# A delta-rule kernel with a GELU network behind it: the first group's 32x32 inverses by halves, and two chunks' K work moved

## The chip, the cores and the metric

The kernel runs on one core of a Trainium2 chip. The time is device time of one execution, in microseconds (us). The engines are PE (TensorE, matrix products), DVE (VectorE), ACT (ScalarE), POOL (GpSimd) and SP (SyncE, which issues most of the transfers).

## The reference

Four batches of eight heads run the delta rule over 768 steps with vectors of 48, and the result, with the heads side by side, goes through two matrix products with an exact GELU between them.

```python
# q, k, v: (4, 8, 768, 48), beta: (4, 8, 768)
k_n = k / (np.linalg.norm(k, axis=-1, keepdims=True) + 1e-06)
for t in range(S):
    y[:, :, t] = einsum('bhd,bhde->bhe', q[:, :, t], state)
    v_old = einsum('bhde,bhd->bhe', state, k_n[:, :, t])
    state = state + beta_t * einsum('bhd,bhe->bhde', k_n[:, :, t], v[:, :, t] - v_old)
x = y.transpose(0, 2, 1, 3).reshape(3072, 384)
h = x @ w_in                     # 384 -> 2048
g = 0.5 * h * (1 + erf(h / sqrt(2)))
out = g @ w_out                  # 2048 -> 384
```

The weights arrive as 64-bit floats (two 32-bit words each) and are turned into 32-bit floats on the core.

## The kernel before

**Chunks.** The 768 steps are cut into 12 chunks of 64. In a chunk the recurrence is a triangular system per head: the Gram products of the keys, scaled, make a strictly lower triangular 64x64 matrix; its inverse (`Zf`) applied to the values (`W`) gives `U` (`solve`), from which follow the output (`use`, `read`) and the next state (`update`, `next_state`). A chunk has two tiles ("units", one per pair of batches), a group two chunks, so 32 inverses of 64x64 per half of the partitions. Chunk 0 has no state before it, so its `W` needs no product with the state (`against_state` is one multiply on POOL there).

**The inverse.** The diagonal 32x32 blocks of a group are laid side by side by a transpose on DVE (`flip`, line 482), scaled (line 487), and inverted in place by elimination: for j = 1 to 30 a product of a column with a row (line 494) and an add (line 496), each instruction waiting for the one before. Then two 32x32 inverses become a 64x64 one (`join`, lines 531 to 556): level 0 multiplies the block below the diagonal (`Gs`, here G) by one inverse, level 1 by the other. `XM` holds the inverse turned one way, `Zf` the other; `back` (lines 502 to 509) turns them on DVE.

**The network.** Chunk c's rows, turned (`turn`), go through `fc1` (16 tiles f of the first layer, psH) and `fc2` (psO), the latter adding over f. In chunk 0 the first layer runs while the pieces of w_in are decoded: `begin`, `exponents`, `mantissas` and `signed` work on DVE and ACT, one piece per two tiles f, eight for w_in, then eight for w_out; pieces 0 to 2 have one DVE instruction more (line 260) than 3 to 7. The psH tiles share two PSUM buffers, each freed by a GELU on ACT.

**The order.** Up to `by_hand.close()` (line 1138) the program order is written out by hand for all engines: the chunk 0 and 1 products, the elimination of the first group (`rows`, line 1099), the join and chunk 0's recurrence. While DVE eliminates, PE does the query products of chunks 0 and 1 and, from line 1089 on, the K transposes, Grams and Q transposes of chunks 2 and 3. After it a list of steps with due times (`plan`, in chunk numbers: 1.25 is a quarter into chunk 0's network) sets DVE's order; a scheduler orders PE and ACT from what each instruction waits for. There `join` of chunk 1 stands at 1.085 and 1.16, chunk 1's recurrence at 1.31 to 1.58 (`state_at(1, ...)`), the loads of chunk 3 at 0.98. SP issues transfers in order, and each waits for its buffer.

Of the kernel before, what the change touches and what calls it, by code (L numbers as in the profile page):

```python
# [19 lines left out]
def kernel(  # L20
# [179 lines left out]
    slots = [su.tile([128, 2 * WG], U32, tag=f"w_raw{i}", name="w_raw", bufs=1) for i in range(3)]  # L200
# [329 lines left out]

    def join(g, ts, level, copy=nc.scalar.copy):
# [149 lines left out]
    def solve(us, copies=(nc.scalar.copy, nc.scalar.copy)):  # L681
        psU = dn("psU")
        for u in us:
            zf = Zf[(u.c // 2) % 2]
# [368 lines left out]
    for n in range(2):  # L1053
        fetch(n)
    load_k(2, "Kp")
    new_group(0)
# [3 lines left out]
    for u in first:  # L1060
        squares(u, n0[:, u.t], nc.gpsimd if u.t == 1 else nc.vector)
        transposed(u, (0,))
        if u.t in (1, 2):
            diagonals(first[u.t - 2 + 1])
    diagonals(first[2])
    signs(0, 2)
    diagonals(first[3])
    root(n0)
    scales_, flip_, *rows, back0, back1, back2, clear_ = [s_[1:] for s_ in eliminate_steps(0)]
    factors(gms[0], beta_m[:, 0:2].rearrange("q c a h -> q (c a) h"), n0)  # L1070
    scales_[0]()
    flip_[0]()
# [4 lines left out]
    for u in first:  # L1077
        transposed(u, (1,))
        queries([u])
    for a in range(NA):  # L1080
        fetch_in(tiles[2, a].Qp[:, :, 0:D], q, tiles[2, a])
    for a in range(NA):
        fetch_in(Qp[2 + a][:, :, 0:D], k, tiles[3, a])
    for n in range(2, NS):
        fetch(n)
    for n in range(n_in, n_in + len(slots)):
        fetch(n)
    load_v(1)
    third = [tiles[2, a] for a in range(NA)]
    for u in third:  # L1090
        transposed(u, (0,))
    grams(third)
    for u in third:
        transposed(u, (1,))
    fourth = [tiles[3, a] for a in range(NA)]
    for u in fourth:
        transposed(u, (0,))
    grams(fourth)
    for fn, *args in rows:
        fn(*args)  # L1100
    nc.vector.scalar_tensor_tensor(ng, gms[0][:, 0:NA], -1.0, ns[0], ALU.mult, ALU.mult)
    back0[0](*back0[1:])
    against_state(first[:NA])
    for u in first:
        masked(u)
    back1[0](*back1[1:])
    for a in range(NA):
        join(0, (a,), 0)
    back2[0](*back2[1:])
    for a in range(NA):  # L1110
        join(0, (a,), 1)
    clear_[0](*clear_[1:])
# [5 lines left out]
    begin(1)  # L1118
    mantissas(1)
    solve(first[:NA])  # L1120
    exponents(1)
    signed(0)
    use(first[:NA])
    for u in first[:NA]:
        read(u)
# [170 lines left out]
```

## Time and profile before

| | |
|---|---|
| median of 3 runs | 646.93 us (646.61 to 647.02) |
| the profiled execution | 647.82 us, its span 645.8 us |
| PE busy in the span | 621.7 us (96%) |
| DVE busy | 499.2 us (77%) |
| ACT busy | 260.3 us (40%) |
| POOL busy | 63.4 us (10%) |
| chunk 0's first layer (psH) starts | 57.64 us |
| second layer (psO) starts | 90.40 us |

Lines of a timeline give start and length in us, the engine, the source line, the operation, what is written from what, the form, and in brackets how long the engine had been idle before and what released it. A group's line gives count, total time, the mean of one in ns and the idle time before. A chain's line gives start, length, engine, what, and the line. Records of PE count the passes of 32-bit products, so one 32-bit matmul makes two records and one transpose makes one.

### The profile page before, as it was taken

To read this page: it belongs to the slowest core of one execution; us is meant where nothing else is said; L and a number is where in the kernel's file an instruction comes from. 1 tells how busy PE (TensorE), PEld (TensorE's weight loads), DVE (VectorE), ACT (ScalarE), POOL (GpSimd) and SP (SyncE) were. 2 spreads that over 40 slices of the span, in tenths; PEclk is the share of its full clock that TensorE was granted. 3 is DMA by queue.
4 is the path that set the end of the run, shared out by engine and by line. 5 is a ranking of instruction groups with operands and counts; after the bars stand their busy time and mean duration, and the time that the engine had idled before them with its cause. 6 is when DMAs were issued, how large, how long until landed. Compare 5 with 4: busy or idle time off the path is not lost.

```text
span 645.8 us, 22160 instructions
## 1 busy us (share of the span) xinstructions
PE 621.7 (96%) x9702; PEld 574.4 (89%) x9702; DVE 499.2 (77%) x1023; ACT 260.3 (40%) x586; POOL 63.4 (10%) x58
## 2 busy tenths in 40 slices
PE   6769999999999999999999999999999999999997
PEld 5657776776699999999999999999999999999997
DVE  6999889989799997999677999677999565354342
ACT  3366777625352157132156132166132253132230
POOL 4041004100311004001004001003001000000000
PEclk9976999999899999999999999999999999999999
DMA  9795654303433235321425312412211300100101
GB/s 129 178 272 170 127 159 138 50 1 69 63 59 46 53 44 88 54 30 31 70 34 84 60 25 36 71 18 38 51 25 34 67 5 3 25 2 2 26 3 24
DMA packets 158433, 39.79 MB, mean 62 GB/s; under 512 B 150016, under 2 KB 153216, under 8 KB 158336
## 3 DMA queue, kind: packets, MB, share of 16 engines
q1 hardware_dynamic: 155344, 36.94, 29.5%
q10 hardware_dynamic: 2992, 1.43, 1.1%
q8 instruction: 76, 1.25, 0.8%
q14 instruction: 21, 0.17, 0.1%
HBM read 33.62 MB, written 4.72 MB: 59 GB/s over the span
## 4 chain that ended last, share of the span: by engine, by line
PE 86%; DVE 8%; ACT 2%; issue 2%; DMA 1%; ACTq 0%; SPq 0%; DVEq 0%
PE psX L834 12%; PE psY L889 11%; PE psX L889 8%; PE psY L834 7%; PE psO L804 7%; PE psH L786 6%; PE psV L889 5%; PE psZ L889 5%; PE psZ L834 4%; PE psV L834 4%; PE psK L660 3%; PE psG L414 3%; PE psJ L586 2%; DVE tmp L494 2%; DVE Nu L496 2%; PE psU L690 2%
## 5 line engine op out<-in xcount | busy, mean ns | idle before, releaser
L494 DVE TENSOR_TENSOR tmp<-Nu 128x30 f32<-128x30 f32 (+9 forms) x180 | 62.0, 345 | 4.7
L496 DVE TENSOR_TENSOR Nu<-Nu,tmp 128x30 f32<-128x30 f32 (+9 forms) x180 | 60.3, 335 | 6.2
L889 PE MATMUL psX<-xT,w_in_sb 128*128 128x128 f32 x480 | 64.6, 277 | 0.5 <-DVE p L986 0.4
L889 PEld LDWEIGHTS psX<-xT,w_in_sb 128*128 128x128 f32 x480 | 58.8, 192 | 1.9 <-issue 0.7
L877 ACT COPY xT<-psX 128x768 f32<-128x768 f32 x9 | 7.2, 799 | 124.3 <-PE psX L763 124.3
L834 PE MATMUL psX<-w_out_sb,G 128*128 128x192 f32 x320 | 55.3, 326 | 0.0
L351 POOL TENSOR_TENSOR n<-n,half 128x16 f32<-128x16 f32 x10 | 29.9, 2986 | 258.8 <-DVE n L349 205.4
L834 PEld LDWEIGHTS psX<-w_out_sb,G 128*128 128x128 f32 x320 | 52.1, 190 | 0.0
L804 PE MATMUL psO<-w_out_sb,G 128*128 128x384 f32 x128 | 46.4, 508 | 0.0
L786 PE MATMUL psH<-xT,w_in_sb 128*128 128x256 f32 x192 | 44.6, 386 | 1.9 <-ACT G L877 1.8
L786 PEld LDWEIGHTS psH<-xT,w_in_sb 128*128 128x128 f32 x192 | 36.1, 192 | 8.7 <-ACT G L877 2.9
L889 PE MATMUL psY<-xT,w_in_sb 128*128 128x128 f32 x320 | 42.3, 275 | 0.0
L877 ACT COPY pu<-psZ 128x512 f32<-128x512 f32 x40 | 23.5, 587 | 39.2 <-PE psZ L889 39.2
L889 PEld LDWEIGHTS psY<-xT,w_in_sb 128*128 128x128 f32 x320 | 38.9, 192 | 0.0
L804 PEld LDWEIGHTS psO<-w_out_sb,G 128*128 128x128 f32 x128 | 24.1, 196 | 14.9 <-issue 1.7
L877 ACT ACTIVATE G<-G 128x512 f32<-128x512 f32 x40 | 25.2, 630 | 18.6 <-DVE G L920 17.8
L376 POOL TENSOR_TENSOR V<-V,n 128x384 f32<-128x384 f32 x18 | 16.0, 898 | 133.5 <-DMA V<-in_v_dram 131.9
L834 PE MATMUL psY<-T,G 128*128 128x192 f32 x160 | 28.6, 332 | 0.0
L834 PE MATMUL psZ<-T,pu 128*128 128x192 f32 x160 | 28.6, 332 | 0.0
L912 DVE TENSOR_TENSOR psY<-psY,pu 128x512 f32<-128x512 f32 x20 | 14.0, 698 | 18.0 <-PE psY L889 18.0
L834 PE MATMUL psV<-w_out_sb,G 128*128 128x192 f32 x160 | 27.7, 326 | 0.0
L834 PE MATMUL psX<-T,G 128*128 128x192 f32 x160 | 27.6, 326 | 0.0
(178 smaller groups left out, 1347.3 us busy)
## 6 DMA issues: line engine op xcount, KB each, us to landing
Kp<-in_k_dram SPq DMA_DIRECT2D x76, 96.0 KB, 3.3
w_out_sb<-in_moe_w_in_dram SPq DMA_DIRECT2D x24, 256.0 KB, 4.5
w_raw<-in_moe_w_out_dram SPq DMA_DIRECT2D x16, 384.0 KB, 4.4
V<-in_v_dram SPq DMA_DIRECT2D x48, 96.0 KB, 3.1
out_dram<-o_sb SPq DMA_DIRECT2D x36, 96.0 KB, 2.2
Qp<-in_q_dram SPq DMA_DIRECT2D x64, 32.0 KB, 2.1
Qp<-in_q_dram SPq DMA_DIRECT2D x16, 96.0 KB, 3.9
Qp<-in_k_dram SPq DMA_DIRECT2D x32, 32.0 KB, 2.3
```

Source lines behind the costliest of these rows:

```text
L351: nc.gpsimd.tensor_tensor(flat, flat, half, op=ALU.pow)
L376: engine.tensor_tensor(u.V, u.V, ns[u.c][:, u.a].unsqueeze(2).to_broadcast([128, H, D]), op=ALU.mult)
L414: nc.tensor.matmul(psG[HALF[p], r, i * NP + j, :], lhsT=u.Kt[rows, p, j, :], rhs=(u.Qt if x else u.Kt)[rows, p, j, :], start=True, stop=True)
L494: nc.vector.tensor_tensor(tmp, nu[:, j + 1:, j:j + 1].to_broadcast([128, n, j]), nu[:, j:j + 1, 0:j].to_broadcast([128, n, j]), op=ALU.mult)
L496: nc.vector.tensor_tensor(nu[:, j + 1:, 0:j], nu[:, j + 1:, 0:j], tmp, op=ALU.add)
L660: nc.tensor.matmul(u.psK[to, x, r, j, :], lhsT=(u.Qt if x else u.Kt)[rows, p, j, :], rhs=St[rows, u.a, p ^ r, j, :], start=True, stop=True)
L786: nc.tensor.matmul(psH, lhsT=w_in_sb[:, f // 2, m, f % 2 * 128:(f % 2 + 1) * 128], rhs=xTs[c][:, m, :], start=(m == 0), stop=(m == NM - 1))
L804: nc.tensor.matmul(u.psO, lhsT=G[:, u.a, f, :], rhs=w_out_sb[:, f, :], start=(f == 0), stop=(f == NF - 1))
L834: nc.tensor.matmul(ps_, lhsT=lhs[:, f, :], rhs=rhs[:, f, :], start=first and f == 0, stop=f == FH - 1, skip_group_check=not first)
L877: tc.keep_in_program_order(fn(*args, **kw))
L889: nc.tensor.matmul(ps_[:, i], lhsT=lhs[:, f // 2, f % 2 * 128:(f % 2 + 1) * 128], rhs=rhs, start=first and i == 0, stop=True, skip_group_c ...
L912: nc.vector.tensor_tensor(L1["Y1"], L1["Y1"], L1["pu"][:, 0], op=ALU.add)
```

## The change

The first group alone gets a new inverse. Its 32x32 blocks are cut into 16x16 squares. A tile `N0`, zeroed at the start, holds both squares of a block, and `eliminate_first` runs j = 1 to 14 on the two at once (two free dimensions more in the access pattern). The block between the two squares is then joined by PE: `below` (one 32x16 product per block), `below_out` (a multiply into `M`, whose other half is zero), `corner` (two kinds of products, psB and psC), `corner_out` and `corner_turned` (adds on DVE into `XM` and `Zf`, two copies on ACT). `corner_turned` also fills the left half of `Zf`, which was a transpose (`back`, x = 2). After that `join` runs as before.

Around it the hand-written order changes. The clears of `Zf` go from POOL to ACT, early. Only the first group's chunk 0 is joined at once; chunk 1's `below` is put behind chunk 0's solve, its corner and its join into the plan (1.005 to 1.16). `solve` of chunk 0 gets a PSUM tile for each unit, and unit 1's copies of U and x go to DVE. Unit 1's state update moves behind the turns. Pieces 1 and 2 of w_in are decoded after the recurrence, piece 1 no longer before it. The K transposes, Grams and Q transposes of chunks 2 and 3, and the query product and mask of chunk 1's second unit, move out of the hole under the elimination into chunk 0's first layer (1.1 to 1.27). On SP all four first pieces of w_in and the values of chunk 1 are fetched before chunk 2's keys; w_out's three first raw pieces share their third buffer with `N0` and wait for it; the loads of chunk 3 go from 0.98 to 1.3.

```diff
-    for n in range(2):
+    for n in range(NS):
         fetch(n)
+    load_v(1)
     load_k(2, "Kp")
+    prepare_first()
...
+        if u.t == 0:
+            clear_first(0, 0)
+            clear_first(0, 1)
+        elif u.t == 2:
+            clear_first(1, 0)
...
-    scales_[0]()
-    flip_[0]()
+    scales_first()
+    flip_first()
...
-    for u in first:
-        transposed(u, (1,))
-        queries([u])
+    transposed(first[0], (1,))
+    transposed(first[1], (1,))
+    queries(first[0:1])
+    transposed(first[2], (1,))
+    queries(first[1:2])
     for a in range(NA):
         fetch_in(tiles[2, a].Qp[:, :, 0:D], q, tiles[2, a])
+    for j in range(1, HS - 1):
+        eliminate_first(j)
+    back_first(0)
+    below(0)
+    back_first(1)
+    slots += [su.tile([128, 2 * WG], U32, tag=f"w_raw{i}", name="w_raw", bufs=1) for i in range(3)]
+    for n in range(n_in, n_in + len(slots)):
+        fetch(n)
+    for u in first[:NA]:
+        masked(u)
+    below_out(0)
+    nc.vector.scalar_tensor_tensor(ng, gms[0][:, 0:NA], -1.0, ns[0], ALU.mult, ALU.mult)
+    against_state(first[:NA])
+    queries(first[2:3])
+    masked(first[2])
+    corner(0)
+    corner_out(0)
+    corner_turned(0)
+    for a in range(NA):
+        join(0, (a,), 0)
+    for a in range(NA):
+        join(0, (a,), 1)
+    transposed(first[3], (1,))
     for a in range(NA):
         fetch_in(Qp[2 + a][:, :, 0:D], k, tiles[3, a])
...
-    third = [tiles[2, a] for a in range(NA)]
-    for u in third:
-        transposed(u, (0,))
-    grams(third)
-    for u in third:
-        transposed(u, (1,))
-    fourth = [tiles[3, a] for a in range(NA)]
-    for u in fourth:
-        transposed(u, (0,))
-    grams(fourth)
-    for fn, *args in rows:
-        fn(*args)
...
-    solve(first[:NA])
-    exponents(1)
+    solve(first[:NA], (nc.scalar.copy, nc.vector.tensor_copy), True)
+    below(1)
     signed(0)
     use(first[:NA])
-    for u in first[:NA]:
-        read(u)
-    signed(1)
+    update(first[0])
+    below_out(1)
+    read(first[0])
+    read(first[1], nc.vector.tensor_copy)
     for u in first[:NA]:
         turn(u)
-    for u in first[:NA]:
-        update(u)
+    update(first[1])
+    begin(1)
     begin(2)
+    exponents(1)
     exponents(2)
+    mantissas(1)
+    signed(1)
     mantissas(2)
     signed(2)
     begin(3)
...
-    plan += [at(0.98, 0.985, [(1.0, load, 3)]),
+    plan += [at(1.3, 1.305, [(1.0, load, 3)]),
+             at(1.005, 1.006, [(1.0, corner, 1)]),
+             at(1.05, 1.051, [(1.0, corner_out, 1), (1.0, corner_turned, 1)]),
+             at(1.1, 1.101, [(1.0, queries, first[3:4]), (1.0, masked, first[3])]),
+             at(1.12, 1.17, gram_steps(2)), at(1.18, 1.23, gram_steps(3)),
+             at(1.25, 1.27, [(1.0, transposed, u, (1,)) for u in third]),
              [(t, (join, 0, range(NA, 2 * NA), level)) for level, t in enumerate((1.085, 1.16))],
```

The new steps that it calls:

```python
def eliminate_first(j):
    nu = squares_of(first_["nu"])            # both 16-squares: 128 x 2 x 16 x 16
    n = HS - 1 - j                           # HS = 16
    ...
    nc.vector.tensor_tensor(tmp, nu[:, :, j + 1:, j:j + 1].to_broadcast([128, 2, n, j]),
                            nu[:, :, j:j + 1, 0:j].to_broadcast([128, 2, n, j]), op=ALU.mult)
    nc.vector.tensor_tensor(nu[:, :, j + 1:, 0:j], nu[:, :, j + 1:, 0:j], tmp, op=ALU.add)

def below(c):                                # FOUR: the four quarters of the partitions
    ps_ = first_["psA", c] = ps.tile([128, NA * H, HS], F32, tag="mlp", name="psA")
    for i, u in enumerate(range(units_of(c).start, units_of(c).stop)):
        for rows in FOUR:
            nc.tensor.matmul(ps_[rows, i, :], lhsT=Ds[0][rows, u, :], rhs=XMs[0][rows, u, 0:HS],
                             start=True, stop=True)

def corner(c):
    ...
    for i, u in enumerate(range(units_of(c).start, units_of(c).stop)):
        for rows in FOUR[::2]:
            nc.tensor.matmul(psB[rows, i, :], lhsT=zf[rows, u, HB:C], rhs=m[rows, u, 0:HS],
                             start=True, stop=True)
    for i, u in enumerate(range(units_of(c).start, units_of(c).stop)):
        for rows in FOUR:
            nc.tensor.matmul(psC[rows, i, :], lhsT=m[rows, u, :], rhs=zf[rows, u, HB + HS:C],
                             start=True, stop=True)

def corner_out(c):
    us, xm, zf = units_of(c), XMs[0], Zf[0]
    for rows in FOUR[::2]:
        nc.vector.tensor_tensor(xm[rows, us, 0:HS], xm[rows, us, 0:HS],
                                first_["psB", c][rows], op=ALU.add)
```

## The prediction

> **What bounds the kernel now.** I read the slices of the span first, then the chain in order of time, then the timelines of PE, DVE and ACT around it, then the groups by form for the price of one instruction. Slices (16.1 us each):
>
> ```profile
> PE   6769999999999999999999999999999999999997
> ...
> DVE  6999889989799997999677999677999565354342
> ...
> PEclk9976999999899999999999999999999999999999
> ```
>
> PE is full from the fourth slice to the end. So the kernel is its opening, about 58 us in which PE is not full, plus a long stretch of PE work. A change of the opening is worth what it moves the start of that stretch, less the PE work it adds. The chain in order of time tells what the opening waits for:
>
> ```profile
> 14.11 1.98 DVE Nu L482
> ...
> 17.44 0.22 DVE tmp L494
> ...
> 39.19 0.19 DVE Nu L496
> ...
> 39.49 2.12 DVE XM L505
> ...
> 47.98 2.07 PE psU L690 x61
> ...
> 57.71 4.46 PE psH L786 x18
> ```
>
> The elimination (lines 494 and 496, 60 instructions end to end) holds 17.44 to 39.38; from its end to the first solve (psU) it is 8.6 us, and 9.7 more to the first layer (psH). PE's timeline gives the marks and the clock:
>
> ```profile
> 31.36 1.97 PE L393 MATMUL psT<-ident,Kp 128*128 128x128 f32 x8
> ...
> 34.91 1.09 PE L393 MATMUL psT<-ident,Qp 128*128 128x128 f32 x8
> 38.08 1.97 PE L393 MATMUL psT<-ident,Qp 128*128 128x128 f32 x8 [2.07 <-ACT Qt L394]
> ...
> 44.45 1.96 PE L541 MATMUL psJ<-Zf,XM 32*32 32x32 f32 x64 [0.81 <-DVE XM L552]
> 47.98 2.03 PE L690 MATMUL psU<-W,Zf 64*64 64x48 f32 x64 [1.57 <-issue]
> ...
> 66.02 1.20 PE L541 MATMUL psJ<-Zf,XM 32*32 32x32 f32 x64
> ...
> 82.04 1.15 PE L690 MATMUL psU<-W,Zf 64*64 64x48 f32 x64
> ...
> 86.89 1.56 PE L786 MATMUL psH<-xT,w_in_sb 128*128 128x256 f32 x6 [0.92 <-ACT G L877]
> ...
> 90.40 1.56 PE L804 MATMUL psO<-w_out_sb,G 128*128 128x384 f32 x4
> ...
> 174.37 0.60 PE L393 MATMUL psT<-ident,Qp 128*128 128x128 f32 x4
> ...
> 176.56 1.16 PE L414 MATMUL psG<-Kt 48*64 48x64 f32 x64
> ```
>
> Eight transposes take 1.97 us at 31.36 and at 38.08, 1.09 at 34.91; so the granted 1.00 shown for the first slices is not to be believed, and the opening runs mostly at half clock. The joins and the solve show the same factor (psJ 1.96 against 1.20, psU 2.03 against 1.15). From 90.40, where the second layer begins, PE never stops until 160, in both orders of instructions. I forecast where that mark goes; what follows it is the same work in almost the same order, and shifts with it.
>
> **1. The elimination.** The 30 steps go; 14 steps on two 16-squares at once come, j = 1 to 14 with 28, 52, 72, 88, 100, 108, 112 elements and back.
>
> ```profile
> L487 DVE TENSOR_TENSOR Nu<-Nu,XM 128x1024 f32<-128x1024 f32 x1 | 1.2, 1224 | 0.1
> ...
> L494 DVE TENSOR_TENSOR tmp<-Nu 128x108 f32<-128x108 f32 x2 | 0.5, 271 | 0.1
> ...
> L494 DVE TENSOR_TENSOR tmp<-Nu 128x30 f32<-128x30 f32 x2 | 0.4, 198 | 0.1
> ```
>
> With 0.03 to 0.04 us between instructions, a pair of 30 elements takes 0.49 us, one of 108 takes 0.61; the seven sizes give 3.9, twice that 7.8, against 21.9. The scaling is two products of 256 (0.45 each, between the 0.41 of 240 elements and a quarter of 1.22) for 1.24. It starts at 14.11 as now, since that waits for ACT's diag copy at 14.08; so it ends at 24.9 instead of 39.4. Three memsets and a reduction (about 1.7 us by the 0.70 of 768 elements) fit DVE's 1.96 us wait for Kp. The four clears of Zf (0.63 each on ACT, for three of 0.69 on POOL and one on ACT) fall into ACT's waits of 1.27, 0.67 and 1.03 us between 6 and 13.7: nothing, unless a K copy is late.
>
> **2. The joins.** XM's transpose (2.13) ends at 27.1. Then new: 64 products 32x16 (128 records), a multiply (0.45), 32 and 64 products (192 records), two adds (0.44) and one (0.45), two ACT copies (0.62). A record's price is not in the trace: psD, four tiles at once, 13 ns; psJ, two tiles, 18 at full and 33 at half clock. I take 13 for the four-tile products and 16 for the others: 1.7 and 2.6 us; ends 1.7 to 4.2 and 2.5 to 6.3. So psA is done at 28.9, M at 29.6, the corner at 32.5, then both old join levels with their four multiplies (0.44) and four copies (0.37): first solve at 36.2 at full clock, 38.0 at half, against 47.98. One transpose of 1.93 is gone. POOL's scaling of the mask is half of its 1.91 and is done before the flip. POOL's masks of chunk 0 now stand ahead of W, from 26 to 28.5, and W waits for ng at 29.7: hidden.
>
> **3. To the first layer.** Chunk 0's U and x copies go half to DVE, one update moves behind the turn; but psA of chunk 1 (1.7) and its corner (2.5) come in on PE, and on DVE 0.95 + 0.95 of copies and a multiply. psH starts at 45.3 (full) to 50 (half) against 57.64.
>
> **4. The new gate.** PE does four tiles of the layer (1.40 each, by 2.79 us for 12 records) and then waits in order for chunk 1's join, which needs chunk 1's corner added on DVE. DVE must first decode pieces 1, 2 and 3: from the x copy at 41.6 on 0.95 + 1.46 + 1.85 + 1.46 + 1.85 + 0.47, the state 0.95, then 1.46 + 0.5 + 0.92, and the adds 0.9: 54.4 at full clock. At half clock the x copy is at 44.7 and the exponents of piece 1 cost 0.8: 58.2. Behind that wait stand queries, transposes, Grams and eleven more tiles' worth of layer; the layer tile f3 waits too, as its PSUM waits for a Gelu that ACT has behind the exponents of piece 3 (at 52). So the 12 us won at psH mostly run into this gate.
>
> **5. The moved K and Gram.** Four K transposes, two Grams, two Q transposes and a query product leave the hole under the elimination for a full PE. By the rows at 174.37 (0.55 from start to start) and 176.56 (1.1): 2.2 + 2.2 + 1.1 + 0.55 = 6.0 us. From the gate to the second layer PE has 12 tiles x 1.40 + joins 2.26 + 6.0 + psK 2.0 + psU 1.1 + psY 1.9 = 30.1 us. ACT gets their copies too: 4 + 2 + 4 + 1 at 0.59, 4 at 0.62, and two turned: 10.2 us on top of 23.5 busy in the 32.8 us from 57.6 to 90.4. Setting the two orders side by side, PE waits three or four times for a copy or a Gelu, 2.9 us in all (2.4 in the same stretch before): 54.4 + 30.1 + 2.9 = 87.4. The PE idle at the gate (2.5 + 1.0 us) is more than the 2 us at 36 to 38 after which the clock fell, so I add 1 us of half clock: 88.4, against 90.40. Bounds: no waits and full clock 84; half clock and waits doubled 94.
>
> **6. Queues.** On SP two pieces of w_in and four loads of V now stand ahead of chunk 2's K, which is wanted only at 56; w_raw's third slot waits for the transpose at 29 and holds up chunk 3's K (wanted at 63) and piece 4 (begun at 52.6). The load of chunk 3 moves behind its last K transpose, some 65; its squares are wanted after 88. Piece 7, for which DVE waited 1.55 us, is fetched earlier against its use. All hidden; were one late, 2 to 4 us by the landing times of 2.1 to 4.5.
>
> **A rule against it.** By single microseconds the clock fell at 38.0, rose at 41.4, fell at 44.9 and rose at 58.7, each after a stretch that was idle or full. The Trainium skill, "TensorE: Matmul & The Clock Gate", Part 1, says the window is free-running, about 3.4 us, and that activity releases the throttle; the trace agrees, 3.4 us apart. By that rule taking filler from PE keeps the opening cold, and the mark would be at 91.2; by the row at 38.08, where work without a gap lifted the clock, the dense stretch from 27.1 lifts it too.
>
> **Rivals.**
> - *Half clock to psH.* The hole from 24.8 to 27.1 speaks for it. 58.2 + 30.1 + 2.9 = 91.2: +0.8 us.
> - *ACT is the bound in the first layer (slower).* It works in order, and has 34 us of work in 33 to 40 us of time; two PSUM tiles per layer leave PE little to run ahead. Half of the 10.2 us in front of Gelus that PE waits for: +5.1 on 88.4 gives 93.5, +3.1 us. It decides (slower by 0.2%) once PE's waits after the gate pass 6.2 us.
> - *All of it.* The gate is earlier (53.5) and nothing waits: 53.5 + 30.1 = 83.6, -6.8 us. Against it: DVE's list before the gate is fixed.
> - *Nothing moves*, since the mark is set by decoding: DVE would reach w_out some 6 us earlier, so no.
>
> **How the numbers follow.** The mark moves by -2.0 us. The profiled run took 647.82 (span 645.8), 0.89 above the median 646.93; it would be 645.8, the median 644.9. Its own range is 642.9 to 646.1. Chances: this 0.47, everything 0.10, half clock 0.15, ACT the bound or a wait I did not see 0.28. 0.2% (1.3 us) is about what a measurement can tell from no change. Faster: 0.43 of the first and the 0.10; same: the rest of the first, and most of half clock; slower: ACT and a little of half clock. The range 641.0 to 650.0 leaves out the ends of both.
>
> **What would show it.** Elimination over by 25, solve near 36 to 38, psH at 45 to 50, then a hole on PE in front of chunk 1's join at 53 to 58 that waits for DVE, and second layer at 88 to 89. Wrong: no such hole, or holes behind ACT's copies of several us, or transposes that still take 1 us for four in the first layer.

## The result, and the profile after

The changed kernel takes 664.75 us (median of 4 runs, 664.62 to 665.26) against 646.77 (646.58 to 647.02) for the kernel before in the same series: a ratio of 1.0279, 95% interval 1.0261 to 1.0297. It is 18 us slower; 644.9 was predicted, and 650.0 was the upper end of the range. The profiled execution took 665.26 us, with a span of 663.2.

The slices of the span (16.6 us each) and the row of the queue that brings PE's instructions, of the profile after:

```profile
PE   5765989999999999999999999999999999999997
...
DVE  7836658998989998799777799777899765455342
...
PEclk9655899999999999999999999999999999999999
...
q8 instruction: 81, 1.33, 0.9%
```

The full stretch on PE begins one slice or so later than before, and the clock row stays low through the third and fourth slices. From there on nothing differs. The loss is in the opening. The timeline of PE after, at the marks of the prediction (start, length, what, and in brackets the idle time before with its releaser):

```profile
29.08 1.91 PE L607 MATMUL psA<-XM,diag 32*32 32x16 f32 x128 [4.66 <-DVE XM L587]
...
34.59 1.58 PE L628 MATMUL psC<-Zf,M 32*32 32x16 f32 x104 [0.46 <-issue]
...
38.73 1.49 PE L655 MATMUL psJ<-XM,G 32*32 32x32 f32 x48 [2.12 <-issue]
40.42 1.96 PE L655 MATMUL psJ<-Zf,XM 32*32 32x32 f32 x64 [0.19 <-DVE XM L666]
...
43.35 0.66 PE L806 MATMUL psU<-W,Zf 64*64 64x48 f32 x10
46.27 1.74 PE L806 MATMUL psU<-W,Zf 64*64 64x48 f32 x54 [2.26 <-issue]
...
50.37 0.94 PE L607 MATMUL psA<-XM,diag 32*32 32x16 f32 x54 [1.19 <-issue]
...
55.06 0.89 PE L834 MATMUL psY<-U,Kp 64*64 64x48 f32 x23 [1.57 <-issue]
...
66.22 1.90 PE L628 MATMUL psC<-Zf,M 32*32 32x16 f32 x128 [4.79 <-DVE St L839]
68.05 7.20 PE L902 MATMUL psH<-xT,w_in_sb 128*128 128x256 f32 x24
75.18 1.24 PE L655 MATMUL psJ<-XM,G 32*32 32x32 f32 x64
...
109.43 1.56 PE L920 MATMUL psO<-w_out_sb,G 128*128 128x384 f32 x4
```

The second layer (psO) starts at 109.43 against 90.40: 19.0 us later, about the whole loss. From chunk 1's join (75.18) to there it is 34.3 us; the prediction had 33.0 for that stretch. So nearly all of the miss lies ahead of the join, forecast at 54.4 and found at 75.18. Three kinds of losses stand between 25 and 75: two long additions on VectorE before 27, five waits of PE without a releaser ("issue", 7.6 us together), and 4.79 us in which chunk 1's corner (psC) waits for a state update on VectorE, with the whole first layer behind it in PE's order.

The first kind, in the timelines of VectorE and POOL after:

```profile
23.56 1.35 DVE L581 TENSOR_TENSOR N<-N,tmp 128x72 f32<-128x72 f32 x1
24.94 0.21 DVE L579 TENSOR_TENSOR tmp<-N 128x52 f32<-128x52 f32 x1
25.19 1.30 DVE L581 TENSOR_TENSOR N<-N,tmp 128x52 f32<-128x52 f32 x1
...
27.02 1.91 DVE L587 STREAM_TRANSPOSE XM<-N 128x1024 f32<-128x1024 f32 x1
```

```profile
23.55 1.27 POOL L453 TENSOR_TENSOR P<-P,mask 128x512 f32<-128x512 f32 x1 [8.24 <-ACT P L447]
25.15 1.26 POOL L453 TENSOR_TENSOR P<-P,mask 128x512 f32<-128x512 f32 x1 [0.34 <-ACT P L447]
```

Two additions of the elimination that take 0.23 us beside an idle POOL take 1.35 and 1.30 here: each starts with a mask product of POOL and ends just after it.

### The profile page after: what moved, and what is told of

Its sections match the earlier page's. It is cut to its first block, busy times and chain, and to the rows that moved or that the text cites. A ratio compares the mean times of both kernels' runs of the same rounds, so it can differ in the third digit from the quotient of the medians.

```text
span 663.2 us, 23425 instructions
## 1 busy us (share of the span) xinstructions
PE 627.8 (95%) x10342; PEld 581.7 (88%) x10342; DVE 492.5 (74%) x1009; ACT 261.3 (39%) x587; POOL 60.1 (9%) x55
## 4 chain that ended last, share of the span: by engine, by line
PE 80%; DVE 10%; ACT 5%; issue 3%; DMA 1%; ACTq 0%; POOL 0%; SPq 0%; DVEq 0%; POOLq 0%
PE psX L950 11%; PE psY L1005 10%; PE psX L1005 8%; PE psY L950 7%; PE psV L1005 5%; PE psZ L1005 5%; PE psO L920 5%; PE psZ L950 4%; PE psV L950 4%; PE psH L902 3%; PE psK L774 3%; PE psG L414 3%; PE psJ L700 2%; PE psY L825 2%; PE psU L806 2%
## 5 line engine op out<-in xcount | busy, mean ns | idle before, releaser
L496 DVE TENSOR_TENSOR Nu<-Nu,tmp 128x30 f32<-128x30 f32 (+9 forms) x150 | 51.4, 342 | 5.2
L494 DVE TENSOR_TENSOR tmp<-Nu 128x30 f32<-128x30 f32 (+9 forms) x150 | 51.0, 340 | 3.7
L902 PE MATMUL psH<-xT,w_in_sb 128*128 128x256 f32 x192 | 47.0, 395 | 2.6 <-ACT G L993 2.3
L920 PE MATMUL psO<-w_out_sb,G 128*128 128x384 f32 x128 | 44.6, 492 | 0.0
L950 PE MATMUL psY<-w_out_sb,G 128*128 128x192 f32 x160 | 27.6, 326 | 0.0
```

What stands on the lines that cost most here:

```text
L494: nc.vector.tensor_tensor(tmp, nu[:, j + 1:, j:j + 1].to_broadcast([128, n, j]), nu[:, j:j + 1, 0:j].to_broadcast([128, n, j]), op=ALU.mult)
L496: nc.vector.tensor_tensor(nu[:, j + 1:, 0:j], nu[:, j + 1:, 0:j], tmp, op=ALU.add)
L902: nc.tensor.matmul(psH, lhsT=w_in_sb[:, f // 2, m, f % 2 * 128:(f % 2 + 1) * 128], rhs=xTs[c][:, m, :], start=(m == 0), stop=(m == NM - 1))
L920: nc.tensor.matmul(u.psO, lhsT=G[:, u.a, f, :], rhs=w_out_sb[:, f, :], start=(f == 0), stop=(f == NF - 1))
L950: nc.tensor.matmul(ps_, lhsT=lhs[:, f, :], rhs=rhs[:, f, :], start=first and f == 0, stop=f == FH - 1, skip_group_check=not first)
```

## The experiments

The theory formed from this profile has four terms: (T1) PE runs out of instructions, about once every 128 matmul records, and in this opening the records are so short that this shows; (T2) chunk 1's corner asks for a PSUM buffer of the pair "dn", both held by psY until the state update; (T3) POOL's masks stop the elimination; (T4) VectorE's decoding of w_in stands in an order that makes it wait. Rivals: the half clock alone; the moved K and Gram work; the price of the new records themselves.

For T1 the profile gives a size: 81 packets of instructions for 10342 matmul records, 127.7 each (before 76 for 9702, the same), 16.4 KB a packet. The five waits stand behind 729, 856, 982, 1110 and 1237 records of PE, that is 126 to 128 apart. Two packets on that queue start at 36.33 and 43.63 us, where PE begins the last weight load that it has before it waits (36.35 and 43.62), take 0.96 and 1.19 us, and PE goes on 1.45 us after each has landed.

The kernel before took 646.15, 648.1 and 646.04 us in the three series of single runs below; 20 runs of it on another chip lay between 644.7 and 648.6. Each kernel up to the block edges ran once. So the marks of the profile are read first, and run times to a microsecond or two.

**Empty records.** The block edges alone are moved.

```diff
+    psE = ps.tile([128, NA * H, HS], F32, tag="mlp", name="psE")
+    for i in range(8):
+        for rows in FOUR:
+            nc.tensor.matmul(psE[rows, i, :], lhsT=Ds[0][rows, i, :], rhs=Ds[0][rows, i, 0:HS],
+                             start=True, stop=True)
     for j in range(1, HS - 1):
         eliminate_first(j)
```

> Edit: 32 more short products (64 records), whose result nobody reads, put into PE's wait of 4.7 us ahead of chunk 0's psA. In the changed kernel PE waits for nothing that the profile shows before records 729, 857, 983, 1110 and 1237 of its own count (0.5, 2.1, 2.3, 1.2 and 1.6 us), 126 to 128 records apart: in psC, in the first join, in psU, in psA of chunk 1, in the first update. Theory 1 (PE gets its code in blocks of 128 records, and short products outrun the fetch): the waits stay at the same counts, so they stand 64 records earlier in the program: in psB, in psC, in the second half of the joins, after psU, in psY. Sum again 6 to 9 us, time 664.7 +- 2. Rival (a wait on another engine that the profile does not resolve): they stay in front of the same products. Rival (the half clock alone makes the opening slow): no change of the waits at all.

PE's timeline of this kernel:

```profile
32.62 1.35 PE L624 MATMUL psB<-M,Zf 32*32 32x16 f32 x44 [0.82 <-issue]
...
36.90 0.73 PE L628 MATMUL psC<-Zf,M 32*32 32x16 f32 x40 [1.75 <-issue]
...
42.39 1.49 PE L655 MATMUL psJ<-Zf,XM 32*32 32x32 f32 x48 [2.21 <-issue]
...
44.86 1.96 PE L806 MATMUL psU<-W,Zf 64*64 64x48 f32 x64
...
47.69 1.79 PE L607 MATMUL psA<-XM,diag 32*32 32x16 f32 x118 [0.55 <-issue]
...
51.30 1.64 PE L825 MATMUL psY<-U,P 64*64 64x48 f32 x52 [1.33 <-issue]
```

The waits left the instructions where they stood: none in the first level of the join, none in the solve (psU), others in psB, in the second level and in the first psY, and that of chunk 1's psA now behind 10 of its records, where it stood behind 74. They stand behind 729, 857, 984, 1110 and 1237 records, the counts of before, so each is 64 records earlier in the work: they belong to the record count. Second layer at 107.37, 662.8 us. T1 holds as a place; its sizes vary from edge to edge (here 0.6 to 2.2 us).

**Chunk 1's corner in a PSUM buffer of its own.**

```diff
-        psC = first_["psC", c] = dn("psC")[:, 0, 0:NA * H * HS].rearrange("q (u n) -> q u n", n=HS)
+        psC = first_["psC", c] = (sq("psC", NA * H, HS) if c else
+                                  dn("psC")[:, 0, 0:NA * H * HS].rearrange("q (u n) -> q u n", n=HS))
```

> Edit: psC of chunk 1 takes a PSUM buffer of the small pool instead of one of the two large ones. Theory 2 (both large buffers hold psY, with the state's sum in it, until DVE's next_state at 65.6 us, behind three pieces of decoding): PE's wait of 4.8 us in front of that psC goes, psC at 61.2 instead of 66.2, psH at 63.1 instead of 68.05; the exponents of piece 3 stand behind the first GELU on ACT, so chunk 1's join comes at about 71 instead of 75.2, the second layer at 105.5 instead of 109.4, time 661 instead of 664.75. Rival (the join is set by DVE's list anyway): psH earlier, join and second layer within 1 us of before, time 664.

```profile
58.80 1.90 PE L629 MATMUL psC<-Zf,M 32*32 32x16 f32 x126
60.63 7.14 PE L903 MATMUL psH<-xT,w_in_sb 128*128 128x256 f32 x24
...
102.58 1.56 PE L921 MATMUL psO<-w_out_sb,G 128*128 128x384 f32 x4
```

The corner follows at once, the layer starts 7.4 us earlier, and the second layer 6.85; 658.3 us. T2 holds, and is the largest single item. It gave more than the 4.8 us of the wait, since the code waits in front of the layer were shorter in that run, 5.5 us for 7.6 (0.89 for 2.26 in the solve, and none in psC).

**Masks behind W on POOL.** `masked` of chunk 0 moves behind `against_state`.

```diff
-    for u in first[:NA]:
-        masked(u)
     below_out(0)
...
     against_state(first[:NA])
+    for u in first[:NA]:
+        masked(u)
     queries(first[2:3])
```

> Edit: POOL's two masks of chunk 0's P stand behind its W products, as in the kernel before. Theory 3 (POOL's masks at 23.5 and 25.2 hold up the DVE adds that run at the same time, 1.36 and 1.31 us instead of 0.26): all 28 steps take 0.2 to 0.3 us, the elimination ends at 24.9 instead of 26.9, everything behind it is 2 us earlier: second layer at 107.4, time 662.8. Rival (the two adds are long for another reason): 26.9 as before, 664.7.

VectorE's timeline has every step at 0.19 to 0.28 us, and the end where the prediction's step put it:

```profile
24.74 0.19 DVE L581 TENSOR_TENSOR N<-N,tmp 128x28 f32<-128x28 f32 x1
24.90 0.09 DVE L586 MEMSET N<- 128x32 f32 x1
25.02 1.92 DVE L587 STREAM_TRANSPOSE XM<-N 128x1024 f32<-128x1024 f32 x1
```

2.0 us are won there; a code wait of 1.01 came into psA, and by 42.97 the solve had 0.4 of it left. The second layer came 3.4 us earlier, 662.13 us; what goes beyond the 2.0 stands beside shorter code waits (0.90 for 2.26 in the solve, 0.19 for 1.57 in the update). The Trainium skill, "SBUF — State Buffer", section "SBUF: two separate sides", says that a VectorE instruction with two SBUF inputs and a GpSimd instruction reading SBUF take a shared pair of ports in turn, the loser blocked for the other's whole length. The two pairs of rows above agree: 23.55 + 1.27 = 24.82 on POOL, and VectorE's 0.23 us of addition end at 24.91. T3 holds.

**Piece 1 decoded before the solve.** `begin`, `mantissas` and `exponents` of piece 1 go back ahead of it.

```diff
     mantissas(0)
+    begin(1)
+    mantissas(1)
+    exponents(1)
     solve(first[:NA], (nc.scalar.copy, nc.vector.tensor_copy), True)
...
-    begin(1)
     begin(2)
-    exponents(1)
     exponents(2)
-    mantissas(1)
     signed(1)
```

> Edit: begin, mantissas and exponents of piece 1 stand before chunk 0's solve, as in the kernel before. Theory 4 (the decode list was put in the wrong place: DVE waits 4.8 us for psU with nothing to do, then 3.1 us for the exponents of piece 1, which ACT has behind the copies of xT): the 3.1 us go and 2 us of piece 1 fall into the wait for psU; next_state at 60.5 instead of 65.6, so psC of chunk 1 waits little, psH at 63.5, second layer 4 to 5 us earlier, time 660. Rival (PE is what is late: the solve and the products behind it): under 1 us.

Chunk 1's corner waits 1.47 us, not 4.79; layer at 62.64, second layer at 104.01; 659.83 us. A code wait in psA grew to 3.11. T4 holds, as another way to shorten the wait of T2.

**Chunk 1's joins to 32 behind two tiles of the first layer.**

```diff
-    below(1)
     signed(0)
...
-    below_out(1)
...
-             at(1.005, 1.006, [(1.0, corner, 1)]),
+             at(1.03, 1.031, [(1.0, below, 1)]),
+             at(1.035, 1.036, [(1.0, below_out, 1)]),
+             at(1.047, 1.048, [(1.0, corner, 1)]),
```

> Chunk 1's products with the diagonal squares, its corner and the addition of the corner go from the by-hand opening into the planned list, behind the first two tiles of chunk 0's first layer: 320 matmul records leave the path in front of that layer. If PE's own records at half clock and the code waits of every 128 records set the start of the layer, it starts without 1.9 + 3.6 us of records, without one or two code waits (1.2 to 2.8 us) and without the 4.8 us wait of chunk 1's corner for a PSUM buffer: 55 to 58 instead of 68.05. Rival, DVE's list sets the pace whatever PE does: the layer starts early, but chunk 1's join stays at 72 to 75 and the second layer at 107 to 109. If both hold in part, the join comes at 66 to 70 and the second layer at 101 to 104. The whole: 652 to 660 against 664.75.

```profile
53.41 2.00 PE L902 MATMUL psH<-xT,w_in_sb 128*128 128x256 f32 x6
...
62.83 1.83 PE L624 MATMUL psB<-M,Zf 32*32 32x16 f32 x61 [4.73 <-DVE M L612]
...
109.73 1.56 PE L920 MATMUL psO<-w_out_sb,G 128*128 128x384 f32 x4
```

The rival wins here: the layer starts 14.6 us earlier and the second layer not at all (666.1 us). The multiply into M now stands behind VectorE's whole hand-written list, at 62.35, and PE waits for it in order. A code wait of 2.58 us in the corner and the clock, granted at half from 61.16 to 78.23, take more of the gain. An early start of the layer is worth nothing while something later in PE's order waits for VectorE.

**Chunk 2's K and Gram back under the elimination.** Its K transposes and Gram are put ahead of `eliminate_first`, its loads ahead of w_in's; the diagonal blocks `Ds[0]` go to the region of w_in's pieces 6 and 7, since their own buffer is wanted.

```diff
+    third = [tiles[2, a] for a in range(NA)]
+    for u in third:
+        transposed(u, (0,))
+    grams(third)
     for j in range(1, HS - 1):
         eliminate_first(j)
...
-             at(1.12, 1.17, gram_steps(2)), at(1.18, 1.23, gram_steps(3)),
+             at(1.18, 1.23, gram_steps(3)),
...
```

> Chunk 2's K transposes and Gram go back under the elimination, its loads ahead of w_in's; chunk 3's stay moved. The elimination has a hole of 2.6 us and more on PE, and the first layer is full. If the moved work is paid in full in the first layer, the second layer comes 2.5 to 3 us earlier (106.5 to 107) and the run takes about 662. If it is hidden in waits there, nothing changes (109.4). If its 64 and more records only shift the code waits as the 64 empty records of the first experiment did, the solve and the layer move by 1 to 2 us either way, and the second layer is at 107 to 108.

```profile
29.30 1.66 PE L608 MATMUL psA<-XM,w_in_sb 32*32 32x16 f32 x128 [1.21 <-DVE XM L588]
...
35.97 1.62 PE L625 MATMUL psB<-M,Zf 32*32 32x16 f32 x54 [3.63 <-issue]
```

Second layer at 108.59, 0.84 us earlier; 664.48 us. From the layer's start to the second layer it is 37.95 us against 41.38 after, so 3.4 us of moved work are gone there; but the opening took 2.6 us more. The hole under the shorter elimination did hide that work: psA starts at 29.30 for 29.08, after a wait for VectorE as before. What grew is the code waits behind it, 11.0 us for 7.6 (3.63, 2.94, 2.39 and 2.06 in psB, psC, the join and psY).

**A warm PE.** Three 128x512 products that nobody reads in PE's hole before psA.

```diff
+    psE = ps.tile([128, 512], F32, tag="mlp", name="psE")
+    for i in range(3):
+        nc.tensor.matmul(psE, lhsT=ident, rhs=low.rearrange("q a b -> q (a b)")[:, 0:512],
+                         start=True, stop=True)
     for j in range(1, HS - 1):
         eliminate_first(j)
```

> Three products of 128x512 that nobody reads fill PE's hole of 2.6 us in front of the first product with the 16-squares (1.6 us at full clock, 3.1 at half). Rival of the prediction, the half clock: if the hole is what keeps the clock at half from 27 to 71, the next window after 27 is granted in full, psA takes 1.0 instead of 1.9 us, the joins 1.2 instead of 2.0, and the first solve is at 39 to 40 instead of 43.35. If holes later (waits for code of 0.5 to 2.3 us in every window) keep it at half, the clock stays 0.5 and nothing moves by more than 0.5 us.

The granted clock was full from 29.68 to 36.51, and psA took 1.39 us for 1.91:

```profile
30.42 1.39 PE L607 MATMUL psA<-XM,diag 32*32 32x16 f32 x128
...
39.50 1.65 PE L655 MATMUL psJ<-XM,G 32*32 32x32 f32 x54 [3.44 <-issue]
41.34 1.96 PE L655 MATMUL psJ<-Zf,XM 32*32 32x32 f32 x64 [0.19 <-DVE XM L666]
```

PE reached the join's first level at 35.72 (after: 35.98) though psA had started 1.3 us later, and then waited 3.44 us for code instead of 2.12. The solve came later, 44.27: what the faster array won up to the edge, the longer wait took. It is one run, and at half clock this edge cost between 2.12 and 3.76 us in other kernels here, so it shows that full clock up to the join did not bring the solve forward, and not that the clock never matters. Later waits were shorter in this run, and the second layer came at 108.16; 663.67 us.

**The first three repairs together** (own PSUM buffer, masks late, piece 1 early).

> The three edits together: chunk 1's corner in its own PSUM buffer, chunk 0's masks behind W on POOL, piece 1's decoding ahead of the solve. Alone they brought the second layer 6.85, 3.4 and 5.4 us earlier. If they were independent: 109.43 - 15.65 = 93.8. The first and the third shorten the same wait (4.79 to nothing, and to 1.47), so I expect 3.3 less: 97 (96 to 99), and the run at 652.5 (651 to 655). Rival: PE's records at half clock with their code waits are the next bound and eat the rest: 100 to 102, 656.

```profile
60.70 7.40 PE L903 MATMUL psH<-xT,w_in_sb 128*128 128x256 f32 x24
...
102.28 1.56 PE L921 MATMUL psO<-w_out_sb,G 128*128 128x384 f32 x4
```

They bring 7.15 us at the second layer (657.98 us), hardly more than the first alone (6.85), as the rival had it (100 to 102). No wait for VectorE is left in front of the layer; PE's own records and its code waits (6.7 us from 27 on, one of 3.38 us in psA) fill the time.

**The move alone**, in the kernel before: the K transposes and Grams of chunks 2 and 3 and the Q transposes of chunk 2 go into the plan as in the change (chunk 3's Q transposes move in neither kernel), and the elimination on 32 stays.

```diff
-    for u in third:
-        transposed(u, (0,))
-    grams(third)
-    for u in third:
-        transposed(u, (1,))
...
-    for u in fourth:
-        transposed(u, (0,))
-    grams(fourth)
...
-    plan += [at(0.98, 0.985, [(1.0, load, 3)]),
+    plan += [at(1.3, 1.305, [(1.0, load, 3)]),
+             at(1.12, 1.17, gram_steps(2)), at(1.18, 1.23, gram_steps(3)),
+             at(1.25, 1.27, [(1.0, transposed, u, (1,)) for u in third]),
```

> The kernel before with one part of the change alone: chunks 2 and 3's K transposes, their Grams and chunk 2's Q transposes go from the hole under the elimination into chunk 0's first layer; the elimination on 32-squares stays. If the moved work is paid in full and in nothing else, the first layer still starts at 57.6 and the second 5.5 to 6 us later, at 96 to 96.5: 652.5. If their copies on ACT also hold up Gelus or the clock falls, 98 to 101: 655 to 657. If the first layer's waits hide it, 90.4 to 92. In the first case two thirds of the loss of 18 us belong to the squares and their joins on TensorE.

```profile
57.66 4.15 PE L786 MATMUL psH<-xT,w_in_sb 128*128 128x256 f32 x18
...
96.20 1.56 PE L804 MATMUL psO<-w_out_sb,G 128*128 128x384 f32 x4
```

The layer starts where it did (57.64), the second layer 5.8 us later; 652.33 us, 6.3 above the kernel before. The moved work is paid once: some 4.7 of the 5.8 us are its products, and PE's idle time in the stretch grew by 1.1 us (3.1 for 2.0), in waits for ACT's copies of Kt and for GELUs.

**The split copies alone**, in the kernel before.

```diff
...
-    solve(first[:NA])
+    solve(first[:NA], (nc.scalar.copy, nc.vector.tensor_copy), True)
...
-    for u in first[:NA]:
-        read(u)
+    update(first[0])
+    read(first[0])
+    read(first[1], nc.vector.tensor_copy)
     signed(1)
     for u in first[:NA]:
         turn(u)
-    for u in first[:NA]:
-        update(u)
+    update(first[1])
```

> The kernel before with another part alone: U's and x's copies of chunk 0's second half go to VectorE, the two halves' products get PSUM buffers of their own, and one state update stands behind the turn. If ACT's copies are on the path between the solve and the first layer, that layer starts 0.5 to 1.5 us earlier (56 to 57). If VectorE's list is the path, nothing is won, or 1 to 2 us are lost, since it gets 2 us of copies. The run: 645.5 to 648.5 against 647.

```profile
54.05 1.10 PE L711 MATMUL psY<-U,P 64*64 64x48 f32 x32 [2.40 <-DVE U L699]
```

VectorE had decoding in front of the copy of U, and PE waited 2.40 us for it. Layer at 59.59 (1.95 later), second layer at 92.90; 647.42 us. With that order of decoding the split is a loss.

**Four repairs**: the three, with chunk 1's `below` behind the turned x, its multiply ahead of `mantissas(2)`, its corner at 1.035.

```diff
     update(first[1])
+    below(1)
     begin(2)
     exponents(2)
     signed(1)
+    below_out(1)
     mantissas(2)
...
-             at(1.005, 1.006, [(1.0, corner, 1)]),
+             at(1.035, 1.036, [(1.0, corner, 1)]),
```

> The three edits of the eighth run, and besides chunk 1's product with the diagonal squares goes behind the turned x, its scaling on VectorE ahead of piece 2's mantissas, and its corner behind two tiles of the first layer. So 320 records leave PE's path before the layer or are passed by it in part. If a short record costs some 29 ns with its code, the layer starts at 53 to 55.5 instead of 60.70, and the second at 97 to 100 instead of 102.28, since the 192 records of the corner are paid later at 15 to 29 ns: 653 to 656. If VectorE's list is the pace again, as when the joins alone were moved, 101 to 103.

```profile
58.22 1.15 PE L625 MATMUL psB<-M,Zf 32*32 32x16 f32 x61
...
62.88 0.29 PE L629 MATMUL psC<-Zf,M 32*32 32x16 f32 x3 [2.42 <-issue]
63.10 5.45 PE L903 MATMUL psH<-xT,w_in_sb 128*128 128x256 f32 x12
```

The layer starts at 55.38 as expected, the second layer at 103.43 (661.44 us), not at 97 to 100. VectorE is not the reason: PE waits for it nowhere between the layer's start and the join. The corner's 192 records cost 4.9 us behind the first tile, 58.22 to 63.10, 2.42 of them a code wait. And the clock fell once more: it was granted at half from 61.54 to 68.36, and 12 records of the layer took 5.45 us, where 12 at full clock take 2.86. My first theory of what would follow was wrong, and so was its rival's reason.

**Chunk 1's joins to 32 left out**, on top of the three repairs: no `below(1)`, `below_out(1)`, `corner(1)`, `corner_out(1)`, and no addition in `corner_turned(1)`.

> The three edits, and chunk 1's joins from 16 to 32 left out altogether (its 320 records on PE, one scaling and three additions on VectorE; chunk 1's inverse then lacks its corners). It measures what those records cost. By the price of the prediction, 13 to 16 ns each, the first layer starts 4.2 to 5.1 us earlier (55.6 to 56.5) and the second at 97 to 98. By the price that the opening shows with its waits for code, 29 ns, the first layer starts 9.3 us earlier (51.4) and the second at 92 to 94. If neither moves the second layer by more than 2 us, the joins on PE are not what the rest of the loss is.

```profile
56.52 5.26 PE L904 MATMUL psH<-xT,w_in_sb 128*128 128x256 f32 x18
...
96.69 1.56 PE L922 MATMUL psO<-w_out_sb,G 128*128 128x384 f32 x4
```

Second layer 5.6 us earlier than with the three (651.8 us): 17 ns a record, near the lower price. But the work of chunk 0 had more code waits in this run, 8.0 us from 27 on (2.38, 1.01, 3.76, 0.90). With the three repairs it had 3.3, and the other 3.4 of the 6.7 stood in chunk 1's psA. With 3.3 here too the records would have been worth 10.3 us, or 32 ns each; so the price lies anywhere between 17 and 32. What is plain is the rest: without any join of chunk 1 to 32, and with no wait for VectorE from psA's start to the layer above 0.2 us, the layer starts only 1.1 us earlier than in the kernel before, though the elimination ends 13.9 us earlier (25.44 for 39.38).

**Block edges in the kernel before.** 32, 64 and 96 empty records (16, 32 and 48 products) in PE's wait for ACT ahead of chunk 3's K transposes.

```diff
+    psE = ps.tile([128, NA * H, 16], F32, tag="mlp", name="psE")
+    for i in range(4):
+        for z4 in range(4):
+            four_ = slice(z4 * HB, (z4 + 1) * HB)
+            nc.tensor.matmul(psE[four_, i, :], lhsT=Ds[0][four_, i, :], rhs=Ds[0][four_, i, 0:16],
+                             start=True, stop=True)
     fourth = [tiles[3, a] for a in range(NA)]
```

> The kernel before with 16 short products (32 records) that nobody reads, in PE's wait of 2.07 us for ACT ahead of chunk 3's K transposes: the edges of the 128-record code blocks fall 32 records earlier in the work, and nothing else changes. The wait of 1.57 us in front of psU, with no releaser, stood at record 836, which is psU's first. By the code theory it goes from there into the second level of the join, behind 32 of its 64 records; the solve starts at 47 to 48.2 and the run takes 646 to 647.5. If that wait belongs to psU itself (a semaphore, the clock), it stays in front of it.

> The same with 64 records. The edge falls in front of the second level of the join, where PE waits 0.81 us for VectorE anyway. By the code theory the 1.57 us in front of psU go, 0 to 0.8 come in front of the join, and the solve and the first layer start 0.7 to 1.5 us earlier: 645.4 to 646.3, a little faster than before with 64 records more. If extra short records on this path only cost their own time, 647 to 648.

> The same with 96 records: the edge falls inside the first level of the join, between its two halves, where PE waits 0.51 us for ACT. By the code theory the wait in front of psU goes and 0 to 1.1 us come into the first level: solve at 46.4 to 47.5, 645.4 to 646.8. If the records only cost their own time, 647 to 648.

All three are a little slower than the kernel before, and none is faster: ratios 1.0029 (1.0017 to 1.0042), 1.0020 (1.0002 to 1.0038) and 1.0065 (1.0038 to 1.0091). With 64 records, in PE's timeline:

```profile
48.40 1.59 PE L541 MATMUL psJ<-Zf,XM 32*32 32x32 f32 x50 [1.26 <-issue]
51.51 1.96 PE L690 MATMUL psU<-W,Zf 64*64 64x48 f32 x64 [1.53 <-POOL Zf L523]
```

The edges moved as the theory has it: behind 45, then 14 records of the join's second level, then 46 of the first, 32 apart. But the 1.57 us in front of the kernel before's solve were no edge. They stayed, and two of these traces name their releaser: POOL's clear of Zf (line 523). With 96 records one edge more shows, 1.17 us among the empty records themselves. In the kernel before POOL's row is this:

```profile
47.28 2.18 POOL L523 MEMSET Zf<- 32x512 f32 x3 [1.19 <-DVE Zf L509]
```

The first of its three clears ends at about 48.0, where the solve starts (47.98). The profile of before had shown "issue" for a wait that belonged to another engine; the true edge there lay 14 records further on, inside psU, covered by it. The forecast of a gain rested on that misreading.

**That clear taken away**, in the kernel before: the clears early, and VectorE's third transpose of the inverse replaced by copies on ACT, as in the change.

```diff
+    clear_[0](*clear_[1:])
     ng = wk.tile([128, NA, H], F32, tag="ng", name="ng", bufs=1)
...
-    back2[0](*back2[1:])
+    top_copies(0)                    # two copies, Zf[top, units of chunk 0, 0:32] <- [..., 32:64]
     for a in range(NA):
         join(0, (a,), 1)
-    clear_[0](*clear_[1:])
+    top_copies(1)
```

> The kernel before with the one part of the change that takes work off the solve's path there: VectorE's third transpose of the inverse (1.93 us, 45.23 to 47.16) and the clears behind it on POOL, which the solve at 47.98 waits for, are replaced by early clears and by copies of 0.62 us on ACT. If the solve waits for the clears, it starts at the end of the join's copies on ACT (47.2 to 47.4), 0.6 to 0.8 us earlier, and VectorE's list runs up to 1.9 us earlier; the first layer at 56.5 to 57.2 and the run 0.4 to 1.5 us below before. If ACT's two more copies ahead of the join's come in their place, no change; half a microsecond is less than the runs of that chip can tell.

```profile
46.49 0.67 PE L690 MATMUL psU<-W,Zf 64*64 64x48 f32 x14
47.63 1.72 PE L690 MATMUL psU<-W,Zf 64*64 64x48 f32 x50 [0.47 <-issue]
...
57.06 5.24 PE L786 MATMUL psH<-xT,w_in_sb 128*128 128x256 f32 x18
...
88.96 1.56 PE L804 MATMUL psO<-w_out_sb,G 128*128 128x384 f32 x4
```

The solve starts at 46.49 for 47.98, the second layer at 88.96 for 90.40. The hidden edge shows where it had to be, behind 14 of psU's records. 645.49 us (median of 12) against 646.91 (of 17): ratio 0.9984, 0.9971 to 0.9996. This one part of the change makes a kernel faster than both, by 0.16% of the kernel before.

## Why the prediction was wrong, by its steps

The sum failed in its steps 1 to 3, and most in step 3: the first layer was forecast at 45.3 to 50 and began at 68.05, and so chunk 1's join stood at 75.18 and not at 54.4. What follows the join was forecast right.

The marks add up along the kernels tried. From 90.40 to 109.43 the second layer moved by 19.0 us: 5.8 for the moved work (the move alone), 5.6 for chunk 1's joins to 32 (three repairs with and without them), 7.15 for buffers, masks and the order of decoding (what three repairs bring back), and 0.5 that is left (96.69 against 96.20), the net of all that is won and lost in chunk 0's own inverse and recurrence. Each mark is of one run, and the code waits differ by several us from run to run, so the split is rough, and the 0.5 above all. The elimination's gain (13.9 us in the run without chunk 1's joins) was to show up in that last term; the layer's start got 1.1 of it. In that run the way from the elimination's end to the layer takes 31.1 us (25.44 to 56.52) for 18.3 before, and 8.0 of the 12.8 more are code waits.

- **Step 1, the elimination: its arithmetic was right, its cover wrong.** With the masks out of the way it ends at 24.9 and XM's transpose starts at 25.02, as worked out. The step held POOL's masks for "hidden" and set them at 26 to 28.5, behind the elimination; ACT had the query products ready earlier, they ran at 23.55 and 25.15, and cost 2.0 us. It asked whether POOL would be late, not what POOL does to a VectorE that works beside it.
- **Step 2, the joins: prices near, one term missing.** psA took 1.91 us for 1.7; psB and psC 3.6 without the code wait for 2.6, half clock throughout. (Its 33 ns for psJ at half clock is 31: 64 records in 1.96 us.) What failed is that PE was taken to have its instructions at hand. From 31 to the solve's main part the supply cost 4.8 us (0.46, 2.12, 2.26), and PE also did a query product and a group of four transposes on this path (1.1 us each), which the step did not count. The solve, forecast at 36.2 to 38.0, began at 43.35 and was held inside until 46.27.
- **Step 3, to the first layer (45.3 to 50): the failed step with the largest size.** It listed chunk 1's psA and corner as time on PE, and not their buffers or place in the order. The corner's PSUM came free with the state update, at the very end of VectorE's hand-written list; that and the code waits (1.19, 1.57) and VectorE's wait of 3.08 us for an exponent on ACT put the layer at 68.05. Of these the buffer is the largest: its wait is 4.8 us, and the layer came 7.4 us earlier in the run without it, where the code waits were 2.1 us shorter too.
- **Step 4, the gate: right engine, wrong place.** PE did stop in its order for chunk 1 until VectorE was through pieces 1 and 2, and the step's list is that list. But it stopped at the corner, ahead of the layer, so that not even four tiles were done by then; and the list was counted from an x copy at 41.6 to 44.7 that came at 53.26, as VectorE itself waited 4.83 us for the late solve. Chunk 1's join then had no wait at all (75.18).
- **Step 5, the moved work and the stretch to the second layer: right.** 5.5 us forecast for what the move alone moves (6.0 with a query product), 5.8 measured by itself, waits included; 33.0 forecast from the join to the second layer, 34.3 measured; 2.9 of waits for ACT forecast, 3.2 found (three for a GELU, 2.3; two for Kt, 0.9). The 2.4 that it gave for the stretch before are 2.0 of idle.
- **Step 6, the queues: right.** PE waits for no transfer after 27 us.
- **The rivals.** ACT as the bound did not come: its waits stayed under the 6.2 us that would decide. The half clock came, 27.01 to 71.39, longer than the rival had it; it was priced at 0.8 us. The run with the warm PE speaks against it as the cause up to the solve; what it cost behind the solve no run shows. No rival described the case that did come, beyond "a wait I did not see". Even that case was bounded at +3.1 us, because every rival took the opening to shrink by what the elimination loses.

The Trainium skill, "Runtime: NRT & Kernel Launch", section "Instruction fetch mechanics", says that instructions come in blocks of 256 (16 KiB), that crossing an edge is mostly hidden, and that it is hidden because the sequencer is slower than the fill. The block size agrees: 16.4 KB, 128 matmuls with their 128 weight loads. The rest does not hold here: products of 10 to 30 ns outran the fetch, and an edge that showed cost 0.2 to 3.8 us.

The trace shows what such a wait is made of. Between the five waits of the changed kernel there is one packet each. It starts 1.74, 4.89, 1.22 and 2.22 us after PE has passed the edge before, takes 0.96, 1.19, 1.38 and 1.04 us, and PE goes on 1.44 to 1.50 us after it has landed. That makes 4.15, 7.53, 4.10 and 4.70 us for a block, and PE waits for what its own 126 to 128 records leave of it.

What stays open: why the packet starts 1.2 us after the edge in one block and 4.9 in another. It sometimes starts while PE still has 80 records left (47.49) and sometimes only when it has none (43.63); no run here shows what decides that.

## What to carry to other kernels

Before moving a serial chain from VectorE to many small matmuls, count the matmuls: 640 new records brought five more packets of instructions (81 for 76) into an opening in which no other work covers the wait at an edge. Look up for every product in the moved part which PSUM buffer it takes and who frees it, and for every instruction of POOL which VectorE instruction it will run beside. And try each part of such a change alone: here one part in the kernel before was worth 1.4 us, and the whole cost 18 us.

## What the runs showed of the hardware

- PE's instruction supply: over the kernels here no stretch of 384 matmul records was done in less than 9.4 us, 24 ns each (the run with the corner's own buffer, from psA on), though 128 of them took as little as 1.1 us within a block (the four repairs, from 59.19).
- Products on two 32x32 tiles of PE at once cost twice what they cost on four: at half clock psB 30 ns a record (61 in 1.83 us) and psC 15 (104 in 1.58), in the changed kernel; at full clock 19 (61 in 1.15) and 10 (123 in 1.21), in the four repairs.
- A mask product on POOL held a VectorE addition of 0.2 us for its whole 1.27 us, twice.
- A wait shown as "issue" can be an edge or another engine's semaphore. A shift of the record count by a few dozen tells them apart.
